# Attention and a gated MLP on one core: the value products get a higher scheduling priority

## The chip, the cores and the metric

The kernel runs on one core of a Trainium2 chip. The metric is the device time of one execution in microseconds (us), lower is better. The core has a matrix engine (TensorE, PE in the profile, with its weight loads as PEld), a vector engine (DVE), a scalar engine (ScalarE, ACT), GpSimd (POOL), and SyncE (SP), whose queue issues most DMAs. Each engine takes its instructions in the order of its own queue.

## The reference

Four batches of 768 positions, eight heads of 64. Each position sees itself, the 127 before it, and the first 4 positions (the sinks). The heads' outputs stand side by side as x of width 512 and go through an MLP with a gate.

```python
scores = np.matmul(q, k.transpose(0, 1, 3, 2)) / np.sqrt(64)
keep = (pos[None, :] < 4) | ((rel >= 0) & (rel < 128))      # rel = pos[:, None] - pos[None, :]
a = softmax(np.where(keep, scores, -1e9))
x = np.matmul(a, v)                                          # heads side by side: 4 x 768 x 512
h = np.maximum(x @ w_in, 0.0)                                # width 1024
conv = conv_w[0] * shift_right(h) + conv_w[1] * h + conv_w[2] * shift_left(h)
out = (h * sigmoid(conv)) @ w_out                            # 4 x 768 x 512, all float32
```

## The kernel before

**Attention.** Heads go in pairs, 16 pairs in all (4 batches of 4). A pair has two halves of three tiles of 128 positions. In the program's text one step is one tile of one pair, 96 steps, and each step has three slots. Slot 0 writes `scores` of this step's tile: the products sc on PE (L339 in the first batch; L342 and L343, a high and a low part, in the others), the mask and the row minimum on DVE (L508, L509), the exponential on ACT (L512), the sums on DVE (L514, L515) and the scaling of pe on POOL (L517). Slot 1 writes `transp` of the tile one step back: pe is transposed on PE into pts (L532), copied by ACT into pT (L534), and the two triangles of the band are cut out on POOL (L536, L538); behind the third tile of a half the columns of the sinks are transposed too (tk of L546 and L554, then sT). Slot 2 writes `pv` of the tile two steps back, which does something at the third tile of a half only. It opens one tile px in PSUM (one buffer) and writes the products of pT with the values v (L573): 6 in the first half of a pair, 8 in the second, in twos, since head 0 writes the output partitions 0 to 63 and head 1 the partitions 64 to 127. In the trace each of these is two records. The products with the sinks follow (L576, sT with vsr, or with roomH in the first batch). Then `xout` takes px to x:

```python
        nc.scalar.copy(xH[:, hp, s], px)
        nc.vector.tensor_tensor(out=xL[:, hp, s], in0=px, in1=f(xH[:, hp, s]), op=ALU.subtract)
```

Preparing a pair (tq, tk and trq, trk: transposes of q and k on PE, and their evacuations) is written between the slots.

**MLP.** Its work is cut in 96 units, each of 256 positions and 128 of the 1024 inner columns: 12 products ph (L183) of x with w_in, the gate (ACT L190, L194, L197; DVE L195, L196, L198), g in two parts on POOL (L200, L201), and 6 products po (L210) of g with w_out. The units of one batch are written in pieces of four ph or three po between the slots of the next batch's attention steps; the first chunk of batch 0 already in its second half, and the last batch's units behind everything.

**What sets the order.** The order of the text is not the order on the engines. Each instruction gets a priority number as it is written. When the program is built, a scheduler that reckons with the readiness of inputs and free buffers takes for each engine, among what is ready, the instruction with the lowest number. So the order on every engine is fixed when the program starts, and hardware only waits for semaphores. Tiles tagged h (ph, tq, tk, trq, trk) share two PSUM buffers, sc has two, po two, px one. The sink values of each batch come by small DMAs into vsr (`sink_split`, L388 to L395), between the loads of q, k and v on SP.

Of the kernel before, what the change touches and what calls it, by code (L numbers as in the profile page):

```python
# [31 lines left out]
TRAIL = 2  # L32
NGB = TRAIL + 2
LA = 1
WHEN = list(range(2, 19))


# [23 lines left out]
class Moe:  # L61
# [92 lines left out]
    def need(self, n):  # L154

        while self.done < n:
            self.fetch(self.done + 1)
            self.todo[self.done][2](self.raws[self.done])
            self.done += 1
            self.fetch(self.done + LA)  # L160

# [222 lines left out]
def sink_split(c, m, vsr, b):  # L384

    raw, hi, lo = (m.mp.tile([P, 512], d, tag="st", name=f"sink{n}{b}", bufs=3)[0:NS] for d, n in ((F32, "r"), (F32R, "h"), (F32R, "l")))
    c.nc.sync.dma_start(raw.rearrange("s (h d) -> s h d", d=D), c.v[b].rearrange("h s d -> s h d")[0:NS])
    c.nc.scalar.copy(hi, raw)  # L388
    c.nc.vector.tensor_tensor(out=lo, in0=raw, in1=f(hi), op=ALU.subtract)
    for u in range(3):  # L390
        for part, val in enumerate((hi, hi, lo)):
            for j in range(2):
                r = SR * part + 2 * NS * u + NS * j
                dst, src = (f(x).rearrange("s (g j d) -> s g j d", j=2, d=D)[:, :, j] for x in (vsr[r:r + NS, u], val))
                c.nc.sync.dma_start(dst, src)  # L395


def banded(c):
# [46 lines left out]
    def clear():  # L445
        w = vsr.shape[1] * vsr.shape[2] // 2
        for h in range(2):
            nc.sync.dma_start(f(vsr).rearrange("p u n -> p (u n)")[:, w * h:w * h + w], A.zeros[0:3 * SR, 0:w])
# [29 lines left out]
    def fetch(upto=len(queue)):  # L478

        while free[0] and asked[0] < min(len(queue), upto):  # L480
            free[0] -= 1
            g, nm, half = queue[asked[0]]
            st[g].raw[nm, half] = load_half(c, g, nm, half, c.raw[asked[0] % RAWB])
            asked[0] += 1
# [3 lines left out]
    def scores(g, t):  # L488
        s = st[g]
        lo = 0 if t == 0 else (t - 1) * KW  # L490
        mk = m0 if t == 0 else (m1 if t == 1 else m2)
        cols = slice(NS if t == 0 else 0, KW)
        sm = sms[A.tiles % len(sms)]
        A.tiles += 1
        hf, u = divmod(t, 3)
        if u == 0:
            s.pe[hf] = ap.tile([P, 3, 2, KW], F32, tag="pe", name=f"pe{g}_{hf}")
            if t == 0:
                nc.gpsimd.memset(s.pe[hf][:, 0, :, 0:NS], 0.0)
        pe = s.pe[hf][:, u]  # L500
        pcs = [ps.tile([P, SW], F32, tag="sc", name=f"sc{g}_{t}_{j}", bufs=2) for j in range(2)]
        if t == 0:
            A.scores(s, t, [pc[:, KW:SW] for pc in pcs], lo, lo + P)
        else:
            A.scores(s, t, pcs, lo, lo + SW)
        for j, pc in enumerate(pcs):
            if t:
                nc.vector.copy_predicated(pc[:, KW:SW], before.bitcast(I32), pc[:, 0:P])  # L508
            nc.vector.tensor_tensor_reduce(out=pe[:, j, cols], in0=pc[:, P:SW][:, cols], in1=mk, op0=ALU.add, op1=ALU.min,  # L509
                                           scale=1.0, scalar=3.0e38, accum_out=sm[:, j:j + 1])  # L510
        for j in range(2):
            nc.scalar.activation(pe[:, j, cols], pe[:, j, cols], AF.Exp, bias=sm[:, j:j + 1], scale=-1.0,  # L512
                                 accum_out=sm[:, 2 + 2 * j:3 + 2 * j])
        nc.vector.tensor_reduce(out=sm[:, 6:8], in_=sm[:, 2:6].rearrange("p (j e) -> p j e", e=2), op=ALU.add, axis=mybir.AxisListType.X)  # L514
        nc.vector.reciprocal(sm[:, 8:10], sm[:, 6:8])  # L515
        for j in range(2):
            nc.gpsimd.tensor_scalar(pe[:, j, cols], pe[:, j, cols], sm[:, 8 + j:9 + j], 1.0, ALU.mult, ALU.mult)  # L517
# [40 lines left out]
    def pv(g, t):  # L558

        s = st[g]  # L560
        hp = g % NPAIR
        hf, u = divmod(t, 3)
        if u < 2:
            return
        px = ps.tile([P, 3, P], F32, tag="px", name=f"px{g}_{hf}").rearrange("p t k -> p (t k)")
        first = 3 * hf
        tiles = range(first + 2, max(0, first - 1) - 1, -1)
        for kt in tiles:
            pT = s.pT.pop((kt, hf)).rearrange("p h a k -> p h (a k)")
            lo, hi = max(kt, first), min(kt + 1, first + 2)  # L570
            cols = slice(P * (lo - kt), P * (hi - kt) + P)
            for j in range(2):
                nc.tensor.matmul(px[D * j:D * j + D, P * (lo - first):P * (hi - first) + P], s.v[:, kt, j, :], pT[:, j, cols],  # L573
                                 start=(kt == tiles[0]), stop=False, skip_group_check=True)
        for w in range(1 - hf, 3):
            nc.tensor.matmul(px[:, P * w:P * w + P], (vsr if g >= NPAIR else c.vs)[:, w, P * hp:P * hp + P], s.sT, start=False, stop=(w == 2),  # L576
                             skip_group_check=True)
        A.xout(g, hf, px)
# [3 lines left out]
    def prep(n):  # L582

        g, half = jobs[n]
        if g >= NPAIR and half:
            return []
        if g >= PLAIN:
            return A.prep(g, st[g], ahead)
        if half == 0 and g % 2 == 0:
            kks.append(f(ap.tile([P, 4, T, KW], F32R, tag="kk", name=f"kk{g}")))  # L590
        out = []
        for h in (half, half + 1)[0:1 + g // NPAIR]:
            out += A.prep32(g, h, st[g], kks[g // 2][:, g % 2], "po" if g < NPAIR and h == 0 else "h", ahead)
        return out

    def values(n):
        g, half = jobs[n]
        if g < NPAIR:
            st[g].v = load_v(c, g, n % 2, *((2, T) if half else (0, 3)))
        elif half == 0:  # L600
            st[g].v = load_v(c, g, g % 2)

    def coming(n):

        last = 2 * NPAIR - 2
        if n < last:
            return [(n + 1, -0.4, 1.8)]
        if n == last:
            return [(n + 1, -0.4, 1.4), (n + 2, 1.4, 5.6)]
        return [(n + 2, -0.4, 5.1)] if n % 2 == 0 and n + 2 < len(jobs) else []  # L610
# [8 lines left out]
    steps = [(n, g, 3 * half + u) for n, (g, half) in enumerate(jobs) for u in range(3)]  # L619
    NST = len(steps)  # L620
    NSTB = NPAIR * T
    D1, D2 = 1, 2
# [7 lines left out]
    for i in range(NST + D2):  # L630
        if i < NST:
            n, g, t = steps[i]
            if t % 3 == 0:
                for n1, lo, hi in coming(n):
                    new = prep(n1)
                    todo += [(i + lo + (hi - lo) * (k + 1) / len(new), x) for k, x in enumerate(new)]
            if g >= NPAIR or t % 3 == 2:
                fetch()
            if t == 0 and g and g % NPAIR == 0:
                after = i + 3 if g > NPAIR else i  # L640
            if i == after:
                sink_split(c, m, vsr, g // NPAIR)
            if n + 1 < len(jobs) and (t % 3 == 2 if n < 2 * NPAIR else t == 3):
                values(n + 1)
        if i == NSTB // 2:
            clear()
        m.need(min(sum(i >= w for w in WHEN), len(m.todo)))
        for slot in range(SLOTS):
            if slot == 0 and i < NST:
                scores(g, t)  # L650
            if slot == 1 and 0 <= i - D1 < NST:
                transp(*steps[i - D1][1:])
            if slot == 2 and 0 <= i - D2 < NST:
                pv(*steps[i - D2][1:])
                if i - D2 + 1 in cuts:
                    while fill:
                        fill.pop(0)()
                    lo, hi, span = cuts[i - D2 + 1]
                    fill = m.pieces(lo, hi)
                    rate = len(fill) / (span - 0.5)  # L660
                    acc = 0.0
            acc += rate / SLOTS
            while acc >= 1.0 and fill:
                fill.pop(0)()
                acc -= 1.0
            while todo and i + (slot + 1) / SLOTS >= todo[0][0]:
                todo.pop(0)[1]()
# [73 lines left out]
def attention_gated_mlp(ctx: ExitStack, tc: tile.TileContext, q, k, v, n_sink, window, w_in, conv_w, w_out, out):  # L741
# [33 lines left out]
    with tc.If(fast == 1) as cmp:  # L775
        with ExitStack() as es:
            c.es = es
            banded(c)
# [32 lines left out]
```

## Time and profile before

| | us |
|---|---|
| median of 3 runs | 489.43 (487.89 to 490.92) |
| the profiled execution | 490.03 |
| its span, first to last instruction | 488.3 |
| PE busy | 457.4 (94%) |
| PEld busy | 389.7 (80%) |
| DVE busy | 348.4 (71%) |
| ACT busy | 340.5 (70%) |
| POOL busy | 312.7 (64%) |

A matmul's record lasts longer than the distance to the next one, because matmuls are pipelined; so the sum of the records' lengths is not PE's time, and the end of one record to the end of the next is the better measure of what one costs. Idle time in front of an instruction is put down to the last thing that it waited for. The groups of rows further down name engine, line, operation and tile.

### The profile page before, as it was taken

Reading aid. Unit: us, or ns where it says so; the run is one execution under the profiler, and the core shown is the slowest. Engines: PE = TensorE matmul, PEld = TensorE weight load, DVE = VectorE, ACT = ScalarE, POOL = GpSimd, SP = SyncE. Lnnn points to the kernel's source line nnn. Section 1 sums busy time; section 2 is a strip of 40 time slices with the busy share of each in tenths; the row PEclk is TensorE's granted clock in tenths of the full one; section 3 lists DMA queues with packets and bytes.
Section 4 is the critical chain, followed back from the end, with each engine's and each line's share of the span. In section 5 each row is a group of like instructions: output and inputs, shape, how many; then the busy total and the mean of one; then the engine's idle time right before and its main releaser. Section 6 shows DMA issues by size and latency. Waiting matters only on the chain.

```text
span 488.3 us, 10470 instructions
## 1 busy us (share of the span) xinstructions
PE 457.4 (94%) x3149; PEld 389.7 (80%) x3149; DVE 348.4 (71%) x1212; ACT 340.5 (70%) x1086; POOL 312.7 (64%) x614
## 2 busy tenths in 40 slices
PE   2887798899999999999999999999999999999995
PEld 2555477688889888888888888888888888999993
DVE  4798989957968777786677585886675665656553
ACT  3887858778878977786877786876776754545451
POOL 3584796867976867684758577685764564344441
PEclk9988989999999999999999999999999999999998
DMA  5778653537234132334132332324021100101011
GB/s 147 211 229 212 172 168 79 126 85 188 67 72 116 61 83 66 87 96 99 60 77 58 85 81 60 70 63 98 24 55 33 44 3 0 44 2 44 1 44 53
DMA packets 87307, 41.03 MB, mean 84 GB/s; under 512 B 80160, under 2 KB 80184, under 8 KB 87240
## 3 DMA queue, kind: packets, MB, share of 16 engines
q1 hardware_dynamic: 87096, 39.99, 31.5%
q8 instruction: 28, 0.46, 0.4%
q14 instruction: 39, 0.32, 0.2%
q10 hardware_dynamic: 144, 0.26, 0.2%
HBM read 27.60 MB, written 6.29 MB: 69 GB/s over the span
## 4 chain that ended last, share of the span: by engine, by line
PE 80%; DVE 7%; DMA 3%; issue 3%; ACT 2%; POOL 2%; SPq 1%; DVEq 0%; ACTq 0%; POOLq 0%
PE po L210 27%; PE ph L183 26%; PE px L573 8%; PE sc L342 4%; PE pts L532 4%; PE sc L343 3%; PE px L576 2%; PE tq L276 2%; PE tk L294 2%; PE sc L339 2%; POOL pe L517 1%; DVE sc L508 1%; DMA wi_1r<-in_moe_w_in_dram 1%; DVE pe L509 1%; DVE stm L113 1%
## 5 line engine op out<-in xcount | busy, mean ns | idle before, releaser
L210 PE MATMUL po<-woH,g 128*128 128x512 f32 x384 | 142.0, 409 | 1.2 <-POOL g L200 1.0
L183 PE MATMUL ph<-xH,wiH 128*128 128x258 f32 (+1 forms) x384 | 112.2, 292 | 1.2 <-ACT X L255 1.2
L183 PE MATMUL ph<-xH,wiL 128*128 128x258 f32 (+1 forms) x384 | 109.0, 284 | 0.0
L183 PE MATMUL ph<-xL,wiH 128*128 128x258 f32 (+1 forms) x384 | 108.8, 284 | 0.0
L517 POOL TENSOR_SCALAR pe<-pe,sm 128x132 f32<-128x132 f32 (+1 forms) x192 | 82.8, 442 | 34.9 <-DVE sm L515 27.2
L512 ACT ACTIVATE pe<-pe,sm 128x132 f32<-128x132 f32 (+1 forms) x192 | 77.5, 406 | 15.8 <-DVE sm L509 14.7
L200 POOL TENSOR_SCALAR g<-t 128x256 fp32r<-128x256 f32 x96 | 42.2, 439 | 70.7 <-DVE t L198 50.8
L195 DVE SCALAR_TENSOR_TENSOR t<-hb,cw,t 128x256 f32<-128x256 f32 x96 | 54.0, 562 | 36.6 <-ACT t L194 36.1
L201 POOL TENSOR_TENSOR g<-t,g 128x256 fp32r<-128x256 f32 x96 | 75.2, 784 | 5.6
L210 PEld LDWEIGHTS po<-woH,g 128*128 128x128 f32 x384 | 68.7, 189 | 11.6 <-POOL g L200 2.6
L183 PEld LDWEIGHTS ph<-xH,wiH 128*128 128x128 f32 x384 | 73.0, 190 | 5.5 <-ACT X L255 1.6
L210 PE MATMUL po<-woL,g 128*128 128x512 f32 x192 | 76.4, 398 | 0.0
L183 PEld LDWEIGHTS ph<-xH,wiL 128*128 128x128 f32 x384 | 72.9, 190 | 2.1
L183 PEld LDWEIGHTS ph<-xL,wiH 128*128 128x128 f32 x384 | 72.8, 190 | 0.7
L197 ACT ACTIVATE t<-t 128x256 f32<-128x256 f32 x96 | 40.1, 418 | 33.8 <-DVE t L196 33.4
L198 DVE SCALAR_TENSOR_TENSOR t<-t,hb 128x256 f32<-128x256 f32 x96 | 47.5, 494 | 20.1 <-ACT t L197 19.0
L508 DVE COPY_PREDICATED sc<-before,sc 128x128 f32<-128x128 int32 x160 | 45.6, 291 | 22.6 <-PE sc L343 19.1
L509 DVE CUSTOM_DVE_ANT_0 pe<-sc,m 128x132 f32<-128x132 f32 (+1 forms) x192 | 54.0, 288 | 10.3 <-PE sc L343 7.8
L190 ACT ACTIVATE hb<-ph 128x258 f32<-128x258 f32 (+1 forms) x96 | 37.0, 386 | 31.4 <-PE ph L183 30.7
L536 POOL TENSOR_SCALAR_AFFINE_SELECT pT<-pT 128x256 f32<-128x256 f32 x80 | 38.2, 477 | 31.4 <-ACT pT L534 31.1
L196 DVE SCALAR_TENSOR_TENSOR t<-hb,cw,t 128x256 f32<-128x256 f32 x96 | 54.1, 564 | 4.1
L194 ACT ACTIVATE t<-hb,cw 128x256 f32<-128x256 f32 x96 | 49.2, 513 | 7.7 <-POOL g L201 3.9
(124 smaller groups left out, 930.2 us busy)
## 6 DMA issues: line engine op xcount, KB each, us to landing
raw<-in_q_dram SPq DMA_DIRECT2D x64, 96.0 KB
raw<-in_k_dram SPq DMA_DIRECT2D x64, 96.0 KB
out_dram<-stm SPq DMA_DIRECT2D x23, 256.0 KB
kk<-kk SPq DMA_DIRECT2D x24, 198.0 KB
vraw<-in_v_dram SPq DMA_DIRECT2D x24, 192.0 KB
wi_0r<-in_moe_w_in_dram SPq DMA_DIRECT2D x2, 512.0 KB
wi_1r<-in_moe_w_in_dram SPq DMA_DIRECT2D x2, 512.0 KB
wi_2r<-in_moe_w_in_dram SPq DMA_DIRECT2D x2, 512.0 KB
```

What stands on the lines that cost most here:

```text
L183: nc.tensor.matmul(u.h[:, 0:W], w[:, cc, ff * P:(ff + 1) * P], x[:, cc, t0:t1], start=(i == 0), stop=(i == len(prods) - 1))
L194: nc.scalar.mul(a, prev, cw[:, 0, ff:ff + 1])
L195: nc.vector.scalar_tensor_tensor(out=e, in0=this, scalar=cw[:, 1, ff:ff + 1], in1=a, op0=ALU.mult, op1=ALU.add)
L196: nc.vector.scalar_tensor_tensor(out=a, in0=nxt, scalar=cw[:, 2, ff:ff + 1], in1=e, op0=ALU.mult, op1=ALU.add)
L198: nc.vector.scalar_tensor_tensor(out=a, in0=e, scalar=1.0, in1=this, op0=ALU.add, op1=ALU.mult)
L200: nc.gpsimd.tensor_scalar(u.g[:, 0], a, 1.0, 1.0, ALU.mult, ALU.mult)
L201: nc.gpsimd.tensor_tensor(out=u.g[:, 1], in0=a, in1=f(u.g[:, 0]), op=ALU.subtract)
L210: nc.tensor.matmul(po[:, 0:c.DM], u.g[:, a, tt * P:(tt + 1) * P], w[:, ff, :], start=(ff == 0 and i == 0), stop=(ff == NFF - 1 and i == 2))
L508: nc.vector.copy_predicated(pc[:, KW:SW], before.bitcast(I32), pc[:, 0:P])
L509: nc.vector.tensor_tensor_reduce(out=pe[:, j, cols], in0=pc[:, P:SW][:, cols], in1=mk, op0=ALU.add, op1=ALU.min, scale=1.0, scalar=3.0e38, ...
L512: nc.scalar.activation(pe[:, j, cols], pe[:, j, cols], AF.Exp, bias=sm[:, j:j + 1], scale=-1.0, accum_out=sm[:, 2 + 2 * j:3 + 2 * j])
L517: nc.gpsimd.tensor_scalar(pe[:, j, cols], pe[:, j, cols], sm[:, 8 + j:9 + j], 1.0, ALU.mult, ALU.mult)
```

## The change

`pv` is written under a priority that is 300 numbers lower, in all batches. One step writes about 109 instructions (10470 by 96), so 300 numbers are some three steps: among the instructions that are ready, those of `pv` are taken as if they stood three steps earlier in the text. With it go the products with the values and with the sinks and the two evacuations in `xout`. Nothing is computed in another way.

```diff
 LA = 1
+AHEAD = 300
 WHEN = list(range(2, 19))
...
             if slot == 2 and 0 <= i - D2 < NST:
-                pv(*steps[i - D2][1:])
+                with c.tc.high_priority(offset=AHEAD):
+                    pv(*steps[i - D2][1:])
                 if i - D2 + 1 in cuts:
```

Line numbers behind the new constant are one higher in the changed kernel, and two higher behind the call: L573 is L574 there, L210 is L211. What it does to the order is seen on PE. The first place is the first half of pair 6 (second batch): px_0_2388 is the tile of its value products, and tq the transposes of the next q. Before:

```order
L532 MATMUL pts<-ident,pe_1_2280 128x128 x2
L573 MATMUL px_0_2388<-pT_2_0_2309,vraw_71 64x128 x2
L573 MATMUL px_0_2388<-pT_1_0_2257,vraw_71 64x256
L276 MATMUL tq_2302<-identr,nq_2264 128x128 x3
L573 MATMUL px_0_2388<-pT_1_0_2257,vraw_71 64x256
L573 MATMUL px_0_2388<-pT_0_0_2184,vraw_71 64x256 x2
L554 MATMUL tk_2_2313<-identr,sk_0_2314 72x128
```

In the changed kernel:

```order
L533 MATMUL pts<-ident,pe_1_2280 128x128
L343 MATMUL sc_5_1_2406<-kk_1156,X_2013 128x260
L344 MATMUL sc_5_1_2406<-kk_1156,X_2013 128x260
L574 MATMUL px_0_2388<-pT_2_0_2309,vraw_71 64x128 x2
L574 MATMUL px_0_2388<-pT_1_0_2257,vraw_71 64x256 x2
L574 MATMUL px_0_2388<-pT_0_0_2184,vraw_71 64x256 x2
L555 MATMUL tk_2_2313<-identr,sk_0_2314 72x128
```

The three tq no longer stand between the value products. The second place, also on PE, is where pair 10's second half (px_1_4178) closes; one of its products stands alone, 20 rows behind its group, before:

```order
L573 MATMUL px_1_4178<-pT_3_1_3959,vraw_71 64x256 x2
L573 MATMUL px_1_4178<-pT_2_1_3961,vraw_71 64x128
L532 MATMUL pts<-ident,pe_0_4061 128x128
...
L210 MATMUL po_3684<-woH,g_3926 128x512
L554 MATMUL tk_5_4089<-identr,sk_1_4090 72x128
L573 MATMUL px_1_4178<-pT_2_1_3961,vraw_71 64x128
L342 MATMUL sc_2_1_4214<-kk_1443,X_3835 128x260
```

In the changed kernel:

```order
L574 MATMUL px_1_4178<-pT_4_1_4033,vraw_71 64x256 x2
L574 MATMUL px_1_4178<-pT_3_1_3959,vraw_71 64x256 x2
L574 MATMUL px_1_4178<-pT_2_1_3961,vraw_71 64x128 x2
L533 MATMUL pts<-ident,pe_0_4061 128x128
L343 MATMUL sc_2_0_4213<-kk_1443,X_3835 128x260
```

The lone product stands with its partner. The third place, on PE, is the start of the fourth batch: po takes g_4126, which is the g of unit 41 of the MLP, ph_4243 is unit 43, and px_0_4392 the first half of pair 11. Before:

```order
L183 MATMUL ph_4243<-xL_1687,wiH 128x258
L573 MATMUL px_0_4392<-pT_2_0_4310,vraw_72 64x128 x2
L573 MATMUL px_0_4392<-pT_1_0_4239,vraw_72 64x256 x2
L573 MATMUL px_0_4392<-pT_0_0_4161,vraw_72 64x256 x2
L532 MATMUL pts<-ident,pe_1_4280 128x128 x2
L276 MATMUL tq_4256<-identr,nq_4252 128x128 x3
L342 MATMUL sc_5_1_4421<-kk_1443,X_3951 128x260
L343 MATMUL sc_5_1_4421<-kk_1443,X_3951 128x260
L210 MATMUL po_4229<-woH,g_4126 128x512
L210 MATMUL po_4229<-woL,g_4126 128x512
```

In the changed kernel:

```order
L184 MATMUL ph_4243<-xL_1687,wiH 128x258
L343 MATMUL sc_5_0_4420<-kk_1443,X_3951 128x260
L344 MATMUL sc_5_0_4420<-kk_1443,X_3951 128x260
L211 MATMUL po_4229<-woH,g_4126 128x512
L211 MATMUL po_4229<-woL,g_4126 128x512
L211 MATMUL po_4233<-woH,g_4126 128x512
L211 MATMUL po_4233<-woL,g_4126 128x512
L574 MATMUL px_0_4392<-pT_2_0_4310,vraw_72 64x128 x2
L574 MATMUL px_0_4392<-pT_1_0_4239,vraw_72 64x256 x2
L574 MATMUL px_0_4392<-pT_0_0_4161,vraw_72 64x256 x2
L343 MATMUL sc_5_1_4421<-kk_1443,X_3951 128x260
```

The value products of pair 11 and the three tq stood between unit 43's ph and unit 41's po; now they stand behind that po.

## Rows read from the trace of the kernel before

**Rows 1.** The page: the span, PE's busy time, the chain by engine.

```profile
span 488.3 us, 10470 instructions
...
PE 457.4 (94%) x3149; PEld 389.7 (80%) x3149; DVE 348.4 (71%) x1212; ACT 340.5 (70%) x1086; POOL 312.7 (64%) x614
...
PE 80%; DVE 7%; DMA 3%; issue 3%; ACT 2%; POOL 2%; SPq 1%; DVEq 0%; ACTq 0%; POOLq 0%
```

**Rows 2.** Timeline of PE near 82 us, and the view of tile px.

```profile
82.72 0.49 PE L576 MATMUL px<-sT,roomH 96*128 96x128 f32 x2
...
L573 PE MATMUL px<-pT,vraw x448: 272/379/634, 25.7 to 411.6; 128*64 128x256 f32 x83, 128*64 128x128 f32 x67
```

**Rows 3.** Stretches: length, PE, PEld, DVE, ACT, POOL busy, PEclk, DMA share, GB/s.

```profile
120.00:410.00 290.00, 288.69 (x2106) 251.34 (x2105) 210.44 (x782) 215.68 (x716) 200.64 (x407) 1.00 0.26 66
```

**Rows 4.** Waits of PE, 83 to 410 us: us in total, times, longest.

```profile
PE sc L339 <- DVE sm L509: 1.1, 2, 0.7
PE po L210 <- POOL g L200: 1.0, 2, 0.5
PE sc L339 <- DVE sm L515: 0.6, 1, 0.6
PE px L576 <- DMA vsr<-sinkl: 0.5, 1, 0.5
```

**Rows 5.** Timeline of PE, an unbroken group of 16: start, length, instruction.

```profile
245.39 0.28 PE L343 MATMUL sc<-kk,X 128*128 128x260 f32 x1
245.60 1.52 PE L573 MATMUL px<-pT,vraw 128*64 128x128 f32 x16
247.06 0.39 PE L183 MATMUL ph<-xH,wiH 128*128 128x260 f32 x1
247.28 0.28 PE L183 MATMUL ph<-xH,wiL 128*128 128x260 f32 x1
```

**Rows 6.** Timeline of PE, an unbroken group of 12.

```profile
230.85 0.28 PE L343 MATMUL sc<-kk,X 128*128 128x260 f32 x1
231.06 1.30 PE L573 MATMUL px<-pT,vraw 128*64 128x128 f32 x12
```

**Rows 7.** Timeline of PE, pair 6's first half, broken by three tq.

```profile
160.90 0.38 PE L532 MATMUL pts<-ident,pe 128*128 128x128 f32 x2
161.21 0.86 PE L573 MATMUL px<-pT,vraw 128*64 128x128 f32 x6
162.00 0.45 PE L276 MATMUL tq<-identr,nq 128*128 128x128 f32 x3
162.38 1.08 PE L573 MATMUL px<-pT,vraw 128*64 128x256 f32 x6
```

**Rows 8.** Timeline of PE, the lone product of pair 10's second half.

```profile
273.17 0.22 PE L554 MATMUL tk<-identr,sk 128*72 128x128 f32 x1
273.32 0.43 PE L573 MATMUL px<-pT,vraw 128*64 128x128 f32 x2
273.68 0.39 PE L342 MATMUL sc<-kk,X 128*128 128x260 f32 x1
273.90 0.28 PE L343 MATMUL sc<-kk,X 128*128 128x260 f32 x1
```

**Rows 9.** Timelines of PE and POOL, unit 41: last ph, g, first po.

```profile
276.75 0.28 PE L183 MATMUL ph<-xL,wiH 128*128 128x258 f32 x1
...
285.86 0.64 POOL L200 TENSOR_SCALAR g<-t 128x256 fp32r<-128x256 f32 x1 [2.84 <-DVE sm L514]
...
286.55 0.51 PE L210 MATMUL po<-woH,g 128*128 128x512 f32 x1 [0.51 <-POOL g L200]
```

**Rows 10.** Stretches, columns as in rows 3: before unit 41's g, and the MLP alone.

```profile
280.00:286.00 6.00, 6.00 (x47) 4.85 (x45) 5.75 (x23) 4.92 (x19) 1.95 (x5) 1.00 0.66 191
420.00:440.00 20.00, 20.00 (x126) 18.05 (x125) 11.34 (x22) 8.69 (x21) 8.81 (x15) 1.00 0.00 1
```

## The prediction, made before the changed kernel was run

> **What bounds the kernel now.** I read the page first, then the busy time by stretch, the waits of TensorE, its timeline, and last the built orders of the two programs. The profiled execution took 490.03 us, of which 488.3 us is the span [rows 1]; 1.7 us lies around it, and the median of the three timed runs is 489.43 us. TensorE (PE) holds the chain that ended last for 80% of the span [rows 1]. The two built orders of PE are the same for their first 257 products, of which the last is in the row at 82.72 us, and the same again behind the last group of value products, which started at 411.6 us [rows 2]. So only some 329 us can change. In 120 to 410 us PE is busy for 288.69 of 290 us at a granted clock of 1.00, the upper of its two levels (2.4 GHz) [rows 3]. What it waits for in the stretch that can change is little: the four longest rows hold 3.2 us [rows 4]. So a gain has to come from how the products stand to each other, and a loss from new waits.
>
> **The change part by part.** Nothing is added or removed; PE issues the same products. Four things follow from the two orders.
>
> *Value products that stand together.* A group is 12 records (first half of a pair of heads) or 16 (second half); the 448 of [rows 2] are 16 of each. Each product writes 64 of 128 output partitions, and the two heads run side by side. Undisturbed, 16 records take 1.45 us, from the end of the sc ahead of them (245.39 + 0.28) to their own end (245.60 + 1.52). The ph behind them ends 0.33 us later, while the next ph ends 0.11 us after that one, so leaving a group costs 0.22 us [rows 5]. Undisturbed, 12 records take 1.23 us [rows 6]. Where the scheduler put something between them they take more. With three tq in the middle, the two pieces take 0.79 and 1.01 us, 1.80 against 1.23: 0.57 us more [rows 7]. A lone product that was split off from its partner takes 0.36 us (from 273.39, the end of the tk, to 273.75), and the sc behind it ends 0.32 us later instead of 0.11: 0.57 us for a product that costs nothing inside its group, where its partner runs beside it [rows 8]. In the order before, the 26 groups behind 83 us stand in 33 pieces; in the order of the changed kernel in 26. That is seven breaks in six groups (pair 6 first half, 10 second, 11 second twice, 12 second, 13 first, 15 first), all mended: 7 x 0.56 = 3.9 us, all on the path, since PE is the bound there. Two breaks have rows here; the other five, read in the same way, give 0.45 to 0.72 each, so I keep 3.2 to 4.4 us as bounds. The products with the sinks (sT) stay apart from their group in most cases in both orders and give nothing. Other kinds of neighbours change in number by a few up and down; I bound that by the price of one break, 0.5 us either way, and take nothing.
>
> *New waits of PE.* A product that moves up finds its input later, relative to it. PE takes its queue in order, so what stands behind waits too: scores, transposes, and the MLP of the batch before. The place where the two orders show it best is unit 41 of the MLP (counted from 0), where the attention of the fourth batch starts. Its ph ended at 277.03, its g was ready on GpSimd (POOL) at 286.50, and po began at 286.55 after 0.51 us of idle time [rows 9]. DVE, which feeds that g, was busy for 5.75 of the 6 us before [rows 10]. In the changed order the 12 value products of pair 11 (1.23 us, rows like [rows 6]) and three tq (about 0.2) that stood ahead of this po stand behind it, and a pair of sc (0.24) comes in: 1.2 us less cover. If g comes at the same distance, that wait grows by 1.2 us. Along the whole stretch I laid the work between a product and its input in both orders: it is longer for some units and shorter for others, with the same middle. More I do not know of the rest. From below: all of [rows 4] gone, 3.2 us less. From above: 1.2 us here, and as much as all of [rows 4] again elsewhere, 4.4 us more. I take 2.0 us more: the 1.2 us at unit 41, which both orders show, and 0.8, a quarter of [rows 4], for the rest.
>
> *What goes with them.* The evacuations of a group (a copy on ScalarE, a subtraction on DVE) move with it, at the same offset. In 120 to 410 us ACT is busy for 215.68 and DVE for 210.44 of 290 us [rows 3], so an evacuation a few instructions earlier or later lies beside PE's work, and I cost it at nothing. Where that cover is gone, as in 280 to 286 us, it would delay a g, which is the term above.
>
> *The loads.* SyncE's queue changes in a few rows, where loads of q, k and v change places with the small copies of the sink values. The DMA engines are busy for 0.26 of the time [rows 3], and one wait alone hangs on that queue, 0.5 us of px for vsr [rows 4]; it is inside the bounds.
>
> The sum: 490.0 - 3.9 + 2.0 = 488.1 us for a profiled execution, 1.9 us or 0.4% less; on the median of 489.43 it is **487.5 us**. That is within what a measurement of this kernel can tell from no change, about 1% or 4.9 us.
>
> **The rivals.** *The change moves the wait and not the work.* A group that stands together can also stand at the head of the queue and wait there for its last pT. And preferring does not make a group earlier everywhere: in the orders several open later than before, among them that of pair 6's second half. If every mended group waits as long as its break cost, the 3.9 us are lost again and unit 41 still adds its 1.2: 489.4 + 1.2 = 490.6 us. For it: the first product of a group needs the pT that POOL writes last. Against it: [rows 7, 8] show no idle time ahead of the second pieces, so the breaks did not fill a wait that the profile sees.
>
> *The gate comes too late, and the kernel is slower.* The price is that of unit 41: 1.2 us for a unit whose products move up by that much while its g takes the 9.5 us of [rows 9]. Three batches start in the stretch, with three or four units around each start. From the fourth such unit on the 3.9 us are gone, and with eight the time is 489.4 - 3.9 + 9.6 = 495.1 us. For it: DVE at 5.75 of 6 us [rows 10]. Against it: in the changed order most units keep or gain distance.
>
> *PE has more room than its busy time tells.* A ph lasts 0.28 us in [rows 5] and ends 0.11 us after the one before, so a gap of up to 0.17 us does not show as idle. The loads of weights fill 251.34 of 290 us in the stretch, 87%, but 18.05 of 20 us, 90%, at 420 to 440 us, where only the MLP runs [rows 3, 10]. If the new order brought the first to the second, it would take 290 x (1 - 0.867 / 0.9025) = 11.4 us off: 478 us. Against it: value products load 64 columns, the 128*64 of their rows, not 128 [rows 5], so the share is lower for what is computed and not for gaps. The Trainium skill has a rule that goes this way ("Perfetto Trace Analysis", section "Identifying the Most-Contended Engine"): the busy share of matmuls is a bad measure of the room that is left on TensorE, since they are pipelined, and the busy share of the weight loads is to be used. By that rule the stretch is not full, and the two rows agree that it is below the tail.
>
> **How the numbers follow.** The forecast, 485 to 490 us, gets 0.62; the wait that moves, 490 to 491.8, 0.18; the late gate 0.08, most of it above 494.3; room on PE 0.04; and 0.08 is left for the low end of the forecast's own terms (489.4 - 4.4 - 3.2 - 0.5 = 481.3). So faster by over 1% (below 484.5) is 0.12, within 1% is 0.81, slower by over 1% (above 494.3) is 0.07. The range goes from the upper bound of the mended breaks with a quarter of the waits gone, 489.4 - 4.4 - 0.8 = 484.2, to the moved wait with half of what the waits may still add ((4.4 - 2.0) / 2), 490.6 + 1.2 = 491.8.
>
> **What would show it.** In the profile after, everything up to 83 us stands as before. Each group of value products is one row of 12 or 16 records in the timeline. The stretch from 83 us to the end of the last group is some 2 us shorter, and the wait of po for g at the start of the fourth batch (near 285 us) is about 1.7 us. If the groups are whole and the stretch is not shorter, PE's waits in it have grown by some 4 us, and their rows name what came late. The prediction is wrong in its ground if the time ahead of 83 us or behind the last group changes by more than a microsecond, for nothing moves there.

## The result, and the profile after

The changed kernel takes 485.76 us (median of 13 runs, 485.36 to 487.23) beside 489.43 us of the kernel before in the same job (13 runs, 487.63 to 490.92): a ratio of 0.9927, 95% interval 0.9911 to 0.9942. So it is 0.7% faster, 1.7 us below the forecast of 487.5 us and inside the range. The prediction took its 1.9 us for too little to tell from no change; with 13 runs of each kernel the 3.7 us are clear of it. The profiled execution took 486.11 us, 3.9 us less than the one before.

The page of the changed kernel, as [rows 1]:

```profile
span 484.3 us, 10488 instructions
...
PE 453.9 (94%) x3149; PEld 389.7 (80%) x3149; DVE 348.8 (72%) x1212; ACT 338.7 (70%) x1086; POOL 314.2 (65%) x614
...
PE 78%; DVE 7%; POOL 5%; issue 3%; ACT 3%; DMA 2%; SPq 1%; POOLq 0%; DVEq 0%; ACTq 0%
```

TensorE (PE) issues the same 3149 products and as many loads. It is busy for 3.5 us less (457.4 before), and its loads for as long as before. So 3.5 of the 4.0 us by which the span is shorter came out of the products' own successions, and 0.5 out of idle time. The row of the value products, as in [rows 2]:

```profile
L574 PE MATMUL px<-pT,vraw x448: 272/379/634, 25.5 to 407.5; 128*64 128x256 f32 x82, 128*64 128x128 f32 x68
```

The last of them starts at 407.5 us instead of 411.6: all of the gain is there by the end of the groups. The stretch of [rows 3] holds more work now, 2145 products instead of 2106, at the same granted clock of 1.00:

```profile
120.00:410.00 290.00, 289.45 (x2145) 254.45 (x2142) 214.28 (x791) 216.56 (x727) 203.26 (x409) 1.00 0.27 66
```

The waits of PE from 83 to 410 us, as [rows 4]:

```profile
PE sc L340 <- DVE sm L510: 1.5, 2, 1.1
PE sc L340 <- DVE sm L516: 1.0, 1, 1.0
PE po L211 <- POOL g L201: 0.5, 1, 0.5
PE tk L295 <- ACT hb L191: 0.5, 1, 0.5
```

The four longest hold 3.5 us, where they held 3.2. The two rows of sc grew by 0.8 us in all, near 92 and 97 us; one of the two waits of po for g is gone, and the one of px for vsr.

The timeline of PE around the two groups that [rows 7] and [rows 8] show broken, and around a group of 16 ahead of them (start, length, instruction):

```profile
151.36 0.38 PE L533 MATMUL pts<-ident,pe 128*128 128x128 f32 x2
151.67 1.52 PE L574 MATMUL px<-pT,vraw 128*64 128x128 f32 x16
...
162.38 0.28 PE L344 MATMUL sc<-kk,X 128*128 128x260 f32 x1
162.58 1.30 PE L574 MATMUL px<-pT,vraw 128*64 128x128 f32 x12
...
268.25 0.30 PE L533 MATMUL pts<-ident,pe 128*128 128x128 f32 x1
268.48 1.52 PE L574 MATMUL px<-pT,vraw 128*64 128x128 f32 x16
```

Every group is one row of 12 or 16. From the end of the product ahead to its own end each of the 26 groups takes 1.23 us (12 records: 162.66 to 163.88) or 1.45 us (16 records: 268.55 to 270.00).

**An account of the time.** For this and all later runs I priced each product of PE by how much later it ends than the one before it. The *value time* is that of all value products behind the first six groups, and for each piece what the product right behind it takes over its usual price. The *waits* are, for every other succession of two kinds of product from there to the end of the groups, what a product takes over the middle price of that succession in all runs of this study; they come from the trace, whether it shows them as idle time or not. What is left of the profiled time, less the time at which the first six groups were done, is the rest.

| kernel | pieces | value time | waits to 120 us / behind | profiled time | six groups done at | rest |
|---|---|---|---|---|---|---|
| before | 33 | 43.8 | 6.2 / 2.2 | 490.0 | 82.7 | 355.2 |
| the change | 26 | 39.9 | 6.9 / 1.4 | 486.1 | 83.1 | 354.8 |

Value time fell by 3.9 us, and waits by 0.1 in all: 0.7 more ahead of 120 us and 0.8 less behind. The first six groups were done 0.4 us later, and the rest is 0.4 lower. That sums to the 3.9 us.

### The profile page after: what moved, and what is told of

Read it like the earlier page. It is cut to its first block, busy times and chain, and to the rows that moved or that the text cites. A ratio compares the mean times of both kernels' runs of the same rounds, so it can differ in the third digit from the quotient of the medians.

```text
span 484.3 us, 10488 instructions
## 1 busy us (share of the span) xinstructions
PE 453.9 (94%) x3149; PEld 389.7 (80%) x3149; DVE 348.8 (72%) x1212; ACT 338.7 (70%) x1086; POOL 314.2 (65%) x614
## 4 chain that ended last, share of the span: by engine, by line
PE 78%; DVE 7%; POOL 5%; issue 3%; ACT 3%; DMA 2%; SPq 1%; POOLq 0%; DVEq 0%; ACTq 0%
PE ph L184 27%; PE po L211 26%; PE px L574 7%; PE sc L343 4%; PE sc L344 3%; PE pts L533 3%; POOL pe L518 2%; PE tq L277 2%; PE px L577 2%; PE tk L295 2%; POOL wiL L123 1%; DMA wi_1r<-in_moe_w_in_dram 1%; PE sc L340 1%; DVE sc L509 1%; DVE t L197 1%
## 5 line engine op out<-in xcount | busy, mean ns | idle before, releaser
L211 PE MATMUL po<-woH,g 128*128 128x512 f32 x384 | 142.0, 410 | 0.6 <-POOL g L201 0.5
L518 POOL TENSOR_SCALAR pe<-pe,sm 128x132 f32<-128x132 f32 (+1 forms) x192 | 84.3, 451 | 38.3 <-DVE sm L516 29.3
L196 DVE SCALAR_TENSOR_TENSOR t<-hb,cw,t 128x256 f32<-128x256 f32 x96 | 56.3, 586 | 38.0 <-ACT t L195 37.4
L211 PEld LDWEIGHTS po<-woH,g 128*128 128x128 f32 x384 | 68.7, 189 | 10.9 <-POOL g L201 1.8
L211 PE MATMUL po<-woL,g 128*128 128x512 f32 x192 | 76.3, 397 | 0.0
L199 DVE SCALAR_TENSOR_TENSOR t<-t,hb 128x256 f32<-128x256 f32 x96 | 50.0, 521 | 22.0 <-ACT t L198 21.0
L198 ACT ACTIVATE t<-t 128x256 f32<-128x256 f32 x96 | 40.2, 419 | 32.2 <-DVE t L197 31.7
L197 DVE SCALAR_TENSOR_TENSOR t<-hb,cw,t 128x256 f32<-128x256 f32 x96 | 54.6, 569 | 4.2
L537 POOL TENSOR_SCALAR_AFFINE_SELECT pT<-pT 128x256 f32<-128x256 f32 x80 | 39.7, 496 | 21.2 <-ACT pT L535 21.0
```

The costliest lines, as they stand in the source:

```text
L196: nc.vector.scalar_tensor_tensor(out=e, in0=this, scalar=cw[:, 1, ff:ff + 1], in1=a, op0=ALU.mult, op1=ALU.add)
L197: nc.vector.scalar_tensor_tensor(out=a, in0=nxt, scalar=cw[:, 2, ff:ff + 1], in1=e, op0=ALU.mult, op1=ALU.add)
L199: nc.vector.scalar_tensor_tensor(out=a, in0=e, scalar=1.0, in1=this, op0=ALU.add, op1=ALU.mult)
L211: nc.tensor.matmul(po[:, 0:c.DM], u.g[:, a, tt * P:(tt + 1) * P], w[:, ff, :], start=(ff == 0 and i == 0), stop=(ff == NFF - 1 and i == 2))
```

## Experiments

Theory A: what the change earns is the mended breaks of the groups of value products, about half a microsecond each on TensorE. Theory B: breaks cost nothing, and any new order that shakes off some waits would earn the same. Theory C: the sinks and the evacuations, which come earlier too, are the gain. Each kernel's ratio is to the kernel before on the same chip (medians of 489.88 to 490.56 us). The accounts of all runs stand in one table behind them.

### Four parts of the change

**Values only.** The priority is around the value products alone, no longer around the sink products and the evacuation:

```diff
-                with c.tc.high_priority(offset=AHEAD):
-                    pv(*steps[i - D2][1:])
+                pv(*steps[i - D2][1:])
 ...
         for kt in tiles:
+            with c.tc.high_priority(offset=AHEAD):
                 for j in range(2):
                     nc.tensor.matmul(px[...], s.v[:, kt, j, :], pT[:, j, cols], ...)
```

> Only the products with the values keep the higher priority; the products with the sinks and the two evacuations are written at their usual one. In its order the 32 groups of value products stand in 32 pieces (39 before, 32 in the changed kernel). Theory A (the gain is the mended breaks, about 0.5 us each on TensorE): ratio to before 0.9925, some 3.6 us less, and the time of TensorE in and behind value products is that of the changed kernel, 40.0 us behind 83 us. Theory B (the gain is in waits that went away, since every engine's order changed): anything between 0.990 and 1.005, not tied to the pieces. Theory C (the earlier products with the sinks and the earlier evacuations give it): 1.00.

Measured: 485.27 us, ratio 0.9898 (0.9883 to 0.9914), 26 pieces. Value time is 39.9 us, as theory A said; the time is 1.3 us below what it said, with waits 1.1 us lower than before. Theory C had said 1.00, and theory B does not exclude this time.

**Sinks and evacuation only.** The other part: priority around the loop of sink products and around A.xout, none for the value products (against the kernel before).

```diff
+        with c.tc.high_priority(offset=AHEAD):
             for w in range(1 - hf, 3):
                 nc.tensor.matmul(px[...], ..., s.sT, ...)
+        with c.tc.high_priority(offset=AHEAD):
             A.xout(g, hf, px)
```

> The other part alone: sinks and evacuations keep the higher priority, the products with the values do not. 39 pieces as before, though 1471 of TensorE's 2857 places hold another product than before, as many as in the changed kernel. Theory A: ratio 1.00, within 1 us of before. Theory B: a gain of 1 to 4 us is as likely as with the values, because the order is stirred as much. Theory C: 0.9925.

Measured: 490.5 us, ratio 0.9992 (0.9977 to 1.0006), 33 pieces. The seven breaks stand in five groups, three of which were whole before, and value time is the same 43.8 us: another order with as many breaks takes the same time. Theory C falls: the sinks and the evacuation earn nothing by themselves.

**Opening only** and **all but the opening.** Priority for the first key tile's pair of a group alone, and for all its other pairs alone (one line or the other, against the kernel before):

```diff
+            with c.tc.high_priority(offset=AHEAD) if kt == tiles[0] else nullcontext():   # opening only
+            with c.tc.high_priority(offset=AHEAD) if kt != tiles[0] else nullcontext():   # all but the opening
                 for j in range(2):
```

> Only the first two value products of a group (its opening) keep the higher priority. They run ahead and the rest follows at its usual place: 45 pieces against 39 before. Theory A: six more breaks, 3 us more than before, ratio 1.006. Theory B: no relation to the pieces, 0.992 to 1.004. Theory C: 1.00.

> The opening of a group stands at its usual priority, only the value products behind it have the higher one: a group does not start by preference, but is not broken either, 33 pieces. Theory A: six breaks mended, 3.1 us less, ratio 0.9937. Theory B: no relation to the pieces. Theory C: 1.00.

Measured: opening only 491.21 us, ratio 1.0016 (1.0007 to 1.0026), 39 pieces; all but the opening 486.32 us, ratio 0.9912 (0.9897 to 0.9926), 27 pieces. Both came out below what theory A said, the first by 2 us and the second by 1.2. The value time of the first did rise, by 2.6 us for six pieces more where A had said 3, but its waits behind 120 us fell from 2.2 to 0.2 us; in the second value time fell by 3.5 us and the waits by 1.4. So breaks cost about what A says, and the waits are a second term that goes its own way.

### What a break consists of

The change again, values only again, sinks in the middle and heads apart ran on one chip; sinks between the heads ran on another, with the two runs of the last part.

**The change again** and **values only again**:

> The changed kernel as it is, on the chip of the next three runs, so that values-only can be set beside it. All theories: 0.991 to 0.994 of before, and the 0.8 us more of PE waits near 97 us that its first trace had and that of values-only had not.

> Priority for the value products alone, beside the whole change. If the first difference (0.9898 against 0.9927) is of the kernel: again 1 to 2 us below the change, with no more wait near 97 us than before had. The reason would be that the priority of the sinks and the evacuation adds 0.8 us of waits there (the run with these two alone had it as well) and breaks off a few more sink products. If it was chance: within 0.5 us of the change.

Measured: 486.66 us, ratio 0.9916 (0.99 to 0.9932), and 485.71 us, ratio 0.9902 (0.9884 to 0.992). The medians are 0.95 us apart, the runs overlap (485.4 to 487.07 and 484.93 to 486.36). The difference lies between the 1 to 2 us of the one expectation and the 0.5 of the other. The waits ahead of 120 us came out as expected, 6.9 us in the first and 6.2 in the second. PE's waits from 83 to 120 us in values only, the first run:

```profile
PE sc L340 <- DVE sm L510: 1.1, 2, 0.7
PE sc L340 <- DVE sm L516: 0.6, 1, 0.6
```

These are the figures of [rows 4]; the whole change has 1.5 and 1.0 in the same two rows.

**Sinks in the middle.** The whole change, with the sink products of a group moved in behind its second pair. Every pair stays together, and each group is now two pieces (shortened; the stop flag goes over to the last value products, here and in the next run):

```diff
             for j in range(2):
                 nc.tensor.matmul(px[...], s.v[:, kt, j, :], pT[:, j, cols], ...)
+            if kt == tiles[1]:
+                for w in range(1 - hf, 3):
+                    nc.tensor.matmul(px[...], ..., s.sT, ...)
-        for w in range(1 - hf, 3):
-            nc.tensor.matmul(px[...], ..., s.sT, ...)
```

> The changed kernel, with the two or three sink products of a group put behind its second pair of value products, where they stood behind the last. No product is added and none loses its partner; each of the 26 groups behind 83 us is now two pieces, 52 in all. Theory A (a piece costs about 0.5 us in time to enter and to leave the 64-column products): 26 x 0.48 = 12.5 us more on TensorE in and right behind value products (52 to 53 us, where the change had 40.0), 496 to 499 us, 1.012 to 1.017 of before. A narrower theory A2 (most of the price is the product that a break leaves without its partner, entering and leaving alone are cheap): 2 to 5 us more, 0.996 to 1.003. Theory B (pieces cost nothing, waits make the difference): the change's time within 1 us, 0.991 to 0.995.

Measured: 496.17 us, ratio 1.0129 (1.0098 to 1.016), 52 pieces. The timeline of PE around one group:

```profile
154.86 0.22 PE L555 MATMUL tk<-identr,sk 128*72 128x128 f32 x1
155.01 0.87 PE L574 MATMUL px<-pT,vraw 128*64 128x128 f32 x8
155.81 0.39 PE L343 MATMUL sc<-kk,X 128*128 128x260 f32 x1
156.03 0.28 PE L344 MATMUL sc<-kk,X 128*128 128x260 f32 x1
...
157.79 0.53 PE L578 MATMUL px<-sT,vsr 72*128 72x128 f32 x3
158.25 0.87 PE L574 MATMUL px<-pT,vraw 128*64 128x256 f32 x8
```

The two pieces take 0.80 us each (155.08 to 155.88, 158.32 to 159.12), 1.60 together where a whole group of 16 takes 1.45: 0.15 us to enter 64-column products once more. The sc behind the first piece ends 0.32 us later, the next 0.11: 0.21 us to leave. The account of all 26 agrees: 8.5 us more value time, 0.33 us for each. The Trainium skill ("TensorEngine Tiling (Array Packing)", section "Tiling Modes", under key properties) states that changing the tiling mode, not just the tile, drains the engine; it gives no price, and these rows agree, with 0.15 in and 0.21 us out. The 8.5 us are less than the 12.5 us of theory A and more than the 2 to 5 us of A2; the time falls in A's range only since the first six groups, which are broken too, were done 4.0 us later than in the change again, while the waits are 2.1 us lower in all. Theory B falls here: waits went down, and the time up by 9.5 us.

**Sinks between the heads.** The same, but the sinks stand between the two heads' products of the second key tile, so that a pair is torn as well:

```diff
-            if kt == tiles[1]:
+                if kt == tiles[1] and j == 0:
```

> As the run with the sinks in the middle, but they now stand between the two heads' products of the second key tile, so that each of the 26 groups behind 83 us is broken inside a pair, as some of the groups of before were. Sinks in the middle gave 0.35 us for a break that leaves every pair together. If the rest of the 0.5 us of the kernel before's breaks is the product that loses its partner: a 256-column product on its own in two passes of 0.21 us each, 0.2 to 0.43 us more for each group, 5 to 11 us over the run with the sinks in the middle, 501 to 507 us, 1.023 to 1.035 of before. If a lost partner costs nothing (the rest came from waits): that run's time within 1 us, 1.011 to 1.016.

Measured: 504.39 us, ratio 1.0291 (1.026 to 1.0323), 52 pieces. The timeline of PE around the same group as above:

```profile
155.63 0.38 PE L533 MATMUL pts<-ident,pe 128*128 128x128 f32 x2
155.94 0.86 PE L574 MATMUL px<-pT,vraw 128*64 128x128 f32 x6
...
157.33 0.53 PE L578 MATMUL px<-sT,vsr 72*128 72x128 f32 x3
157.78 1.30 PE L574 MATMUL px<-pT,vraw 128*64 128x256 f32 x10
```

The pieces take 0.79 us (156.01 to 156.80) and 1.22 (157.86 to 159.08), 2.01 in all, 0.41 more than with the pairs whole. In the account it is 10.5 us over sinks in the middle, 0.40 for each of 26, in the first expectation's 5 to 11. So a product of 256 columns that has lost its partner costs about 0.4 us more, and leaving and entering 0.33. One of 128 columns costs half of that: the lone product of [rows 8] takes 0.36 us, 0.21 over the 0.15 to enter.

**Heads apart.** The whole change, with the loop over the heads outside that over the key tiles; the group stays one piece:

```diff
-        for kt in tiles:
-            ...
-            for j in range(2):
+        for j in range(2):
+            for kt in tiles:
+                ...
```

> The changed kernel, with the loop over the two heads outside that over the key tiles: the group is whole, but all products of the first head stand ahead of all of the second. If two neighbouring products of the two heads run side by side in the two halves of TensorE's columns (as the lone product of 0.36 us against a pair's time led me to think), a group of 12 goes from 1.23 to about 2.3 us and a group of 16 from 1.45 to about 2.7, 30 to 38 us in all, ratio 1.055 to 1.07 of before. If they run one after the other anyway: the change's time within 2 us.

Measured: 498.38 us, ratio 1.0165 (1.0143 to 1.0187), from two runs; far outside the first expectation's 1.055 to 1.07 and outside the second's. The timeline of PE around a group of 12 and one of 16:

```profile
120.91 0.28 PE L344 MATMUL sc<-kk,X 128*128 128x128 f32 x1
121.11 1.57 PE L575 MATMUL px<-pT,vraw 128*64 128x128 f32 x12
...
133.19 0.49 PE L295 MATMUL tk<-ident,raw 128*128 128x128 f32 x3
133.61 2.22 PE L575 MATMUL px<-pT,vraw 128*64 128x128 f32 x16
```

The group of 16 takes 2.15 us (133.68 to 135.83) instead of 1.45, and the group of 12 takes 1.50 instead of 1.23 us, where one head behind the other was expected to take 2.7 and 2.3. So the two heads run partly side by side, and not only as neighbours in the queue: about three quarters of what I took for lost comes back in a group of 12, and somewhat under half in one of 16.

### The dose, and the sinks' part

**A lead of 20.** The change with AHEAD = 20 instead of 300:

```diff
-AHEAD = 300
+AHEAD = 20
```

> The change with a lead of 20 instead of 300: too little to win always, so that the scheduler makes 42 pieces of value products, where before had 39 and the change 32. Theory A: 10 pieces over the change at 0.48 us, 4.8 us, and 1.4 us over before: 1.001 to 1.005, if waits stay; with waits 2 us shorter, as the run with the opening alone had, 0.997 to 1.001. Theory C (sinks and evacuations that come earlier by priority are the gain): 0.991 to 0.996, since these still come earlier.

Measured: 492.43 us, ratio 1.0051 (1.0031 to 1.0072), 36 pieces behind the first six groups. This is theory A's case with the waits where they were (8.4 us in both), at the upper end: its ten breaks cost 0.57 each. Theory C had said 0.991 to 0.996; a small lead is worse here than none.

**Values and evacuation.** The whole change without the priority of the sinks:

```diff
-                with c.tc.high_priority(offset=AHEAD):
-                    pv(*steps[i - D2][1:])
+                pv(*steps[i - D2][1:])
 ...
         for kt in tiles:
+            with c.tc.high_priority(offset=AHEAD):
                 for j in range(2):
                     nc.tensor.matmul(px[...], s.v[:, kt, j, :], pT[:, j, cols], ...)
 ...
+        with c.tc.high_priority(offset=AHEAD):
             A.xout(g, hf, px)
```

> Priority for the value products and for the evacuation of their tile, not for the sink products: the whole change but for these. It parts the 0.8 us of PE waits between 83 and 120 us that the change had twice and values-only never: if the sinks' priority makes it, this run has 6.1 to 6.2 us of such waits there, as before, and 0.989 to 0.991 of before; if the evacuation's does, 6.9 us and 0.991 to 0.993.

Measured: 486.04 us, ratio 0.9926 (0.99 to 0.9952). The waits up to 120 us are 6.2 us, as before, so the 0.7 us that the whole change pays there come with the sinks' priority; whether that makes them alone or only beside the evacuation's, no run shows. The ratio lies above the 0.989 to 0.991 expected for this case, and the time doesn't tell the two cases apart.

### All accounts

Times in us, columns as in the table above:

| kernel | pieces | value time | waits to 120 us / behind | profiled time | six groups done at | rest |
|---|---|---|---|---|---|---|
| values only | 26 | 39.9 | 6.2 / 1.1 | 485.1 | 82.6 | 355.3 |
| sinks and evacuation only | 33 | 43.8 | 6.9 / 2.1 | 490.8 | 83.3 | 354.6 |
| opening only | 39 | 46.4 | 6.2 / 0.2 | 490.4 | 82.6 | 355.1 |
| all but the opening | 27 | 40.3 | 6.2 / 0.8 | 485.2 | 82.6 | 355.2 |
| the change again | 26 | 39.9 | 6.9 / 1.6 | 487.1 | 84.0 | 354.7 |
| values only again | 26 | 39.9 | 6.2 / 1.2 | 486.3 | 83.9 | 355.2 |
| sinks in the middle | 52 | 48.4 | 4.4 / 2.0 | 496.8 | 88.0 | 354.1 |
| heads apart | 26 | 53.0 | 5.6 / 1.1 | 499.1 | 84.6 | 354.8 |
| sinks between the heads | 52 | 58.9 | 5.5 / 1.4 | 504.3 | 84.9 | 353.6 |
| a lead of 20 | 36 | 45.6 | 7.4 / 1.0 | 491.7 | 82.7 | 355.1 |
| values and evacuation | 26 | 39.9 | 6.2 / 0.9 | 485.9 | 83.8 | 355.1 |

With before and the change, eleven of the thirteen leave a rest of 354.6 to 355.3 us, and the two that put the sinks into the groups a little less. So value time, waits and the start explain the time of every kernel here to within 1.7 us, and of the eleven to within 0.7. Value time goes from 39.9 to 58.9 us; waits behind the start lie between 6.4 and 9.0.

## Why the prediction was right, point by point

**The mended breaks** were the right step at the right size. Seven breaks at 0.56 us were to give 3.9 us (bounds 3.2 to 4.4), and value time fell by 3.9 (43.8 to 39.9), to the same 39.9 in every run with whole groups in the pairs' order. The two broken groups of [rows 7, 8] and the others are whole. That this is the cause is shown by both directions: parts of the change that leave the breaks leave the time (0.9992 with 33 pieces), and breaks put back cost time again (0.33 where pairs stay whole, 0.73 where one is torn; before's seven, six of which tore a pair, mostly of 128 columns, 0.56 on average). The two prices shown were less alike than they look. The 0.57 of [rows 7] holds the two pieces alone; the first tq behind the first piece ends 0.21 us after it, where a tq's middle price is 0.07, so that break cost 0.71. The 0.57 of [rows 8] does hold what the next product pays. That the mean of these two readings was also that of all seven, whose others cost 0.45 to 0.71, is in part luck.

**New waits of PE** were the term that was mis-sized: 2.0 us more were taken, and 0.1 less came, as a sum of 0.7 more and 0.8 less; that the two nearly cancel was foreseen nowhere. Its sure part was unit 41, where po should have waited for g for about 1.7 us. The timelines of PE, POOL, ACT and DVE in the changed kernel, as [rows 9]:

```profile
276.03 0.28 PE L184 MATMUL ph<-xL,wiH 128*128 128x258 f32 x1
...
279.88 0.46 ACT L198 ACTIVATE t<-t 128x256 f32<-128x256 f32 x1
...
281.35 0.63 DVE L199 SCALAR_TENSOR_TENSOR t<-t,hb 128x256 f32<-128x256 f32 x1
...
282.07 0.41 POOL L201 TENSOR_SCALAR g<-t 128x256 fp32r<-128x256 f32 x1 [0.37 <-DVE sm L515]
...
283.25 0.39 PE L211 MATMUL po<-woH,g 128*128 128x512 f32 x1
284.27 1.30 PE L574 MATMUL px<-pT,vraw 128*64 128x128 f32 x12
```

The same two steps on ACT and DVE before:

```profile
283.19 0.41 ACT L197 ACTIVATE t<-t 128x256 f32<-128x256 f32 x1
...
285.36 0.41 DVE L198 SCALAR_TENSOR_TENSOR t<-t,hb 128x256 f32<-128x256 f32 x1
```

The value products do stand behind this po now, as the order said. But po begins with no idle time ahead of it (no bracket). Its g is ready at 282.48, 6.17 us after the last ph ended at 276.31; before, it took 9.47 (277.03 to 286.50). The failing step is the condition "if g comes at the same distance". The activation on ACT (L198) began 3.57 us after that ph instead of 6.16 (283.19 before), and the product on DVE 5.04 instead of 8.33 (285.36 before): I had compared the order of PE alone, and what ACT and DVE do between ph and g stood in a new order too. The cover was mis-sized as well: PE's work between that ph and this po went from 9.01 us (277.03 to 286.04) to 7.11 (276.31 to 283.42), 1.9 us less instead of 1.2; it did no harm since g came 3.3 us sooner. The 9.47 us were the odd case: the twelve other traces of this study have 4.85 to 7.71 there, and the shortest is that of sinks and evacuation only, in which no value product was preferred.

The other 0.8 us of that term, a quarter of [rows 4], fits the 0.7 more near 92 and 97 us in size, but its place I had not seen. Values and evacuation shows that it comes with the sink products, which I had put at nothing beside the groups. Behind 120 us the waits fell by 0.8 in the change and by up to 2.0 in the other parts of it. Why each of these waits came or went wasn't traced one by one.

**Evacuations and loads** at nothing: right for the loads (no wait for vsr is left in the rows) and for the evacuations as far as runs show: with their priority added to values only, value time is the same 39.9 us and the waits are 7.1 us beside 7.3 and 7.4. No run preferred them alone.

**The rivals.** The wait that moves: no; waits behind 120 us went down by 0.8 instead of up by some 4. The late gate: its site has no wait left, and from 83 to 410 us one wait of po for g is left in all, 0.5 us. More room on PE: the 11.4 us didn't come, but its ground was sounder than I gave it. PE was busy for 288.69 of 290 us in [rows 3], and yet 3.9 us came out of the value products and what follows them, where the profile shows no idle time. The share of the weight loads rose from 251.34 to 254.45 of 290 us, as it had to: all loads together take 389.7 us in both kernels. The Trainium skill ("Perfetto Trace Analysis", section "Identifying the Most-Contended Engine") names that share, beside the share of peak arithmetic, as a better measure of TensorE's room than the matmuls' busy share, and the trace agrees that busy time hid room. By estimate about 8.6 us of entering and leaving (26 groups at 0.33) still lie in the busy time.

**The frame.** The first six groups, whose order did not change, were done at 82.7 us before, and with the changed kernel once at 83.1 and once at 84.0. The second is over the microsecond that the prediction named as a sign against its ground; but values only was at 82.6 once and at 83.9 once, so that much differs between two traces of one kernel, taken on two chips. Behind the groups nothing moved but the time itself. The forecast of 488.1 us for a profiled execution stands against 486.1: 2.1 us of it are the waits, 0.4 the start in the other direction, 0.4 the rest.

**The best version** in these runs is values only: twice 0.99 of before (0.9898 and 0.9902), with the change's value time and 1.0 to 1.1 us less of waits. Against the change itself that is some 0.2%, with overlapping runs; the waits show it, the times do not settle it.

## What to carry to other kernels

Where TensorE is busy all the time, look at how its products follow each other: a run of products in a narrower column mode that is broken by something else costs 0.33 us here for leaving and entering and up to 0.4 more if a product loses the partner that ran beside it, and no view calls that idle. Count the pieces in the built order and price each kind from the timeline, with what the product behind a piece pays; here the prices ran from 0.45 to 0.71 us, and their sum was the fall of the value time, 3.9 us. A wait that hangs on a chain over several engines can't be carried over from one order to the next by looking at one engine's order: lay the orders of all engines of the chain side by side, or give the term no sign.

## What the runs showed of the hardware that I had not expected

Two heads' products that stand far apart in the queue still run partly side by side. With the heads apart, by estimate, one head's eight records of a group of 16 would need 4 x 0.11 + 4 x 0.22 = 1.3 us (the steps between the ends of records of 128 and of 256 columns in that trace), so two heads in a file 2.6 us and the 0.15 to enter; the group took 2.15. A group of 12, by the same steps 2 x 1.1 + 0.15 = 2.3 us, took 1.50. In both groups some records end 0.05 us before the record that started ahead of them, so PE seems to begin the second head's products ahead of the first head's end; since the ends are modelled, how far it reaches ahead stays open.
